# Moving table angles to GpSimd, a weight cast into its transfer and five relus to VectorE, with edge columns padded to 65, in a fused Fourier transform and feed-forward kernel

## The chip, the cores and the metric

The kernel runs on one core of one Trainium2 chip. The metric is the time of one execution on the device, in microseconds (us). The profile shows five engines of the core, each with its own instructions: PE (TensorE, matrix products; PEld is its weight load), DVE (VectorE), ACT (ScalarE), POOL (GpSimd), and SP, which here issues transfers (157 of 128 KB each to the output, among others). They run side by side: in the kernel before, the busy times of PE, DVE, ACT and POOL add up to 1691 us in a span of 628.5 us. All runs named below are on one core.

## The reference

```python
def reference(x, w_in, w_out):          # condensed; x (8, 3008, 256), w_in (256, 2048), w_out (2048, 256)
    X = np.fft.fft(np.fft.fft(x, axis=1), axis=2).real.astype(np.float32)
    h = np.maximum(X.reshape(-1, 256) @ w_in, 0.0)
    return (h * h @ w_out).astype(np.float32)
```

The real part of the transform is C x c - S x s, with cosine and sine matrices C and S over the 3008 positions and c and s over the 256 features. The kernel multiplies c and s into w_in once (G1, G2, G3), so only the transform over the positions is left to do for each of the eight batches, followed by two matrix products, the relu and the square.

## The kernel before

After some 50 us the kernel is a steady stream on PE (busy for 559.84 of the 560 us from 60 to 620 us, at a granted clock of 1.00): xb = G1 * pt + G2 * qt, a relu, a correction with G3, a second relu (both into h), a square, and po = h * wout. The change touches mainly the first 50 us, in which the tables are built and the first batch goes through. The tables are built in two blocks. Each block has two halves, and each half takes five operations on 128x564 elements, on VectorE:

```python
def nk():    vt(m, nval, krow, op=ALU.mult)                                   # L236
def near():  ts(out=t, in0=m, scalar1=1.0 / S, scalar2=R23, ...)              # L240
def turns(): ts(out=t, in0=t, scalar1=R23, scalar2=-float(S), ...)            # L244
def rest():  vt(m, m, t, op=ALU.add)                                          # L248
def size():  absval(t, m)                                                     # L183, on integers
# ... then sines on ScalarE give cosT and sinT, and mirrored columns follow (L279)
```

The second-layer weights arrive as float32 in a staging buffer, and VectorE casts them:

```python
for c in range(4):
    nc.gpsimd.dma_start(out=wot[c], in_=moe_w_out[...])
# ...
def wcast(c): nc.vector.tensor_copy(wout16[:, cs, :], wot[c])                 # L723
spread([(lambda c=c: wcast(c)) for c in range(4)], 3, 7)
spread(rd1[2:], 1, 8)          # the second block's angles
spread(fo, 7, 12)              # v, w: folding the first batch's odd features
# ... the second block's sines and cosines on ScalarE
spread(mi1, 9, 12)             # the second block's mirrored columns
spread(stage1_ops(0, 1, True), 11, 15)   # the second block's transform on PE
```

`spread(ops, lo, hi)` spreads operations over steps lo to hi of the main loop. Each step has one xb group. All relus into h are on ScalarE at this stage:

```python
def x_back(cur):
    # ... xb += G3 * qt
    relu_d(c, u, lambda o, i: act(o, xb[:, :, i], AF.Relu))
```

The edge column of batches 2 to 7 goes through the transform in matmuls with a stationary operand of three columns. There are eight groups of three of them:

```python
(nb, lambda q: eall[k, blk, q, bs[0] : bs[0] + nb], q, cosT)     # nb = 3
```

Of the kernel before, what the change touches and what calls it, by code (L numbers as in the profile page):

```python
# [10 lines left out]
F32 = mybir.dt.float32  # L11
F16 = mybir.dt.float16
I32 = mybir.dt.int32
AF = mybir.ActivationFunctionType
ALU = mybir.AluOpType
# [9 lines left out]
def kernel(  # L25
# [46 lines left out]
    def mm(o, l, r, start, stop):  # L72
        nc.tensor.matmul(o, l, r, start=start, stop=stop, skip_group_check=True)  # L73
# [59 lines left out]
    idx2 = iota("idx2", [P, 1], [[0, 1]], NQ // 2 * (NP - 1), -NQ // 2, I32)  # L133
    wout16 = const.tile([P, NFC, D], F16, name="wout16")
    wst = [h2p.tile([P, 2, F // 4], F32, name="wst", tag="h2") for _ in range(4)]
    wot = [h2p.tile([P, NFC // 4, D], F32, name="wot", tag="h2") for _ in range(4)]
    wS = 2.0 * math.pi / S
    wD = 2.0 * math.pi / D

# [50 lines left out]
    def dmats():  # L190
        pv = nc.gpsimd
        t = tgp.tile([P, P], F32, name="td", tag="td")
        m = tgp.tile([P, P], F32, name="md", tag="md")
        pv.tensor_scalar(out=m, in0=jrow, scalar1=pidx[:, 0:1], scalar2=None, op0=ALU.mult)
        pv.tensor_scalar(out=t, in0=m, scalar1=1.0 / D, scalar2=R23, op0=ALU.mult, op1=ALU.add)
        pv.tensor_scalar(out=t, in0=t, scalar1=R23, scalar2=-float(D),
                         op0=ALU.subtract, op1=ALU.mult)
        pv.tensor_tensor(m, m, t, op=ALU.add)
        pv.memset(csD[:, 0, 0, P - 1 : P], 1.0)

        def fin():
            absval(t, m)
            nc.vector.tensor_copy(csD[:, 0, 1, P - 1 : P], alt)
            act(csD[:, 0, 1, 0 : P - 1], m[:, 0 : P - 1], AF.Sin, bias=0.0, scale=wD)
            act(csD[:, 0, 0, 0 : P - 1], t[:, 0 : P - 1], AF.Sin, bias=hpi[:, 0:1], scale=-wD)

        def hi():
            ts(out=csD[:, 1, :, 0:P:2], in0=csD[:, 0, :, 0:P:2], scalar1=-1.0, scalar2=None,
               op0=ALU.mult)
            nc.vector.tensor_copy(csD[:, 1, :, 1:P:2], csD[:, 0, :, 1:P:2])  # L210
        return fin, hi

    cosT = const.tile([P, NQ, HE + HO], F16, name="cosT")
# [3 lines left out]
    def table_ops(blk):  # L217
        c0, n = BLK[blk]
        ng = (n + 1) // 2
        nm = n // 2  # L220
        cs = slice(c0, c0 + ng)
        tb = {}
        hq = NQ // 2
        kb = krow[:, blk : blk + 1, 0:ng].to_broadcast([P, hq, ng])

        def red(h):
            qs = slice(h * hq, (h + 1) * hq)

            def views():
                return tb["t"][:, qs, 0:ng], tb["m"][:, qs, 0:ng]  # L230

            def nk():
                if h == 0:
                    tb["t"] = tgp.tile([P, NQ, HG], F32, name="tt", tag="tt")
                    tb["m"] = tgp.tile([P, NQ, HG], F32, name="tm", tag="tm")
                vt(views()[1], nval[:, qs].unsqueeze(2).to_broadcast([P, hq, ng]), kb, op=ALU.mult)  # L236

            def near():
                t, m = views()
                ts(out=t, in0=m, scalar1=1.0 / S, scalar2=R23, op0=ALU.mult, op1=ALU.add)  # L240

            def turns():
                t, m = views()
                ts(out=t, in0=t, scalar1=R23, scalar2=-float(S), op0=ALU.subtract, op1=ALU.mult)  # L244

            def rest():
                t, m = views()
                vt(m, m, t, op=ALU.add)  # L248

            def size():  # L250
                t, m = views()
                absval(t, m)

            return [nk, near, turns, rest, size]

        def trig(h):
            qs = slice(h * hq, (h + 1) * hq)

            def cos(qs, bias):
                return lambda: act(cosT[:, qs, cs], tb["t"][:, qs, 0:ng], AF.Sin,  # L260
                                   bias=bias[:, 0:1], scale=-wS)

            def sin(qs, scale):
                return lambda: act(sinT[:, qs, cs], tb["m"][:, qs, 0:ng], AF.Sin, bias=0.0,
                                   scale=scale)

            if h == 0:
                return [sin(slice(0, hq, 2), wS), sin(slice(1, 2), wsh[:, 0:1]),
                        cos(slice(0, 1), hpe), cos(slice(1, 2), hph), cos(slice(2, 3), hpl)]
            return [sin(qs, wS), cos(qs, hpl)]  # L270

        src = slice(c0, c0 + nm)
        dst = slice(c0 + n - 1, c0 + n - 1 - nm, -1)

        def mir(d, a, qs, sv):
            o, i = d[:, qs, dst], (d if qs.start % 2 else a)[:, qs, src]
            if blk == 0:
                return lambda: act(o, i, AF.Copy, bias=0.0, scale=sv[:, 0:1])
            return lambda: ts(out=o, in0=i, scalar1=sv[:, 0:1], scalar2=None, op0=ALU.mult)  # L279

        qg = (slice(0, 5, 4), slice(2, 3), slice(1, 6, 4), slice(3, 4))
        return (red(0) + red(1), trig(0) + trig(1),
                [mir(cosT, sinT, qs, sv) for qs, sv in zip(qg, (nalt, alt, alt1, nalt))]
                + [mir(sinT, cosT, qs, sv) for qs, sv in zip(qg, (nalt, alt, nalt1, alt))])
# [27 lines left out]
        cs = slice(c * 512, (c + 1) * 512)  # L312
        ts(out=G3[:, cs], in0=G2[:, cs], scalar1=s3[:, 0:1], scalar2=None, op0=ALU.mult)

    eall = const.tile([P, 2, NQ, B], F16, name="eall")
    bf = {}
    INL = (0, 1)
    PQ = {}
# [86 lines left out]
    def stage1_ops(b, blk, inline_e=False, run=3):  # L405
# [30 lines left out]
                           (sgn[:, 0:1] if sn and inline_e else None, fin(sn)), run)  # L436
        return ops

    def e_ops(bs):
        nb = len(bs)  # L440

        def start():
            t = esp.tile([4, NK], F16, name="es", tag="es")
            for i, b in enumerate(bs):
                est[b] = (t, i)

        def fin(blk):
            def f(a, bp):
                lo_, hi_ = halves(blk, est[bs[0]][0][0:nb])
                vt(lo_, a, bp, op=ALU.add)  # L450
                vt(hi_, bp, a, op=ALU.subtract)
            return f

        ops = [start]
        for blk in range(2):
            ops += dft_ops(blk, lambda par, blk=blk: [
                (nb, lambda q: eall[k, blk, q, bs[0] : bs[0] + nb], q, cosT)
                for q in range(par, NQ, 2)], nb, (None, fin(blk)))
        return ops

# [24 lines left out]
    def plan(c, y, z):  # L485
        if chunks[c][1] != CH:
            return (), ()
        return ([u for u in range(NFC) if (u * y + 8) % NFC < y],
                [p for p in range(NFC // 2) if (p * z + 4) % (NFC // 2) < z])

    PLAN = [plan(c, *YZ[c]) for c in range(len(chunks))]

    gE = const.tile([P, NFC], F16, name="gE")
# [18 lines left out]
    def mm2_ops(c):  # L512
# [48 lines left out]
        def one(grp, j, fc):  # L561
            s, t0, m = grp[j]

            def f():
                if j == 0 and fc == 0:
                    st["o"] = pso.tile([P, 2, D], F32, name="po", tag="po")
                o = n + n % P + t0 if s == 1 else t0
                w = 2 * m if s == 2 else m
                mm(st["o"][0:w, j, :], h2v(c, fc // nf)[:, fc % (2 * nf), o : o + w], wout16[:, fc, :],
                   fc == 0 and j == 0, fc == NFC - 1)  # L570
                if fc == NFC - 1 and j == len(grp) - 1:
                    return lambda o=st["o"]: store(grp, o)
            return f
# [68 lines left out]
    def x_back(cur):  # L642
        c, u, xb = cur[:3]
        if xb is None:
            return
        g0, n, nf, segs = chunks[c]
        for j in range(nf):
            fs = slice((u * nf + j) * P, (u * nf + j + 1) * P)
            for (b, i, o, l) in segs:
                mm(xb[:, j, o : o + l], G3[:, fs], PQ[b][1][:, i : i + l], False, True)  # L650
        relu_d(c, u, lambda o, i: act(o, xb[:, :, i], AF.Relu))  # L651

    def x_square(cur):
# [19 lines left out]
                          in_=moe_w_in[:, cs].rearrange("(c p) f -> p c f", p=P))  # L673
    for c in range(4):
        nc.gpsimd.dma_start(
            out=wot[c], in_=moe_w_out[c * F // 4 : (c + 1) * F // 4, :].rearrange(
                "(c p) o -> p c o", p=P))
    for h in range(2):
        for f in rd0[5 * h : 5 * h + 5] + (tr0[5:] if h else tr0[:5]):
# [3 lines left out]
    dmats_fin()  # L683
    sgn_vecs()
    nc.vector.memset(ez, 0.0)
    for f in mi0 + fe[0:3] + rd1[0:2]:
        f()
    dmats_hi()
    warm = psx.tile([P, 512], F32, name="warm", tag="x")

    for _ in range(15):
        mm(warm, ez[:, 0, 0, :], ez[:, 0, 0:4, :], True, True)
    for f in fe[3:]:
        f()
    gcast(0, nc.scalar.copy)
    gmat(0)
    for _ in range(3):
        mm(warm, ez[:, 1, 0, :], ez[:, 1, 0:4, :], True, True)
    gcast(1, nc.scalar.copy)
    gcast(2, nc.vector.tensor_copy)  # L700
# [13 lines left out]
    def spread(ops, lo, hi):  # L714
        for i, f in enumerate(ops):
            side.setdefault(lo + int((hi - lo) * i / len(ops)), []).append(f)
# [1 line left out]
    for c in range(1, F // 512):  # L718
        side.setdefault(c * (c - 1) // 2, []).extend([lambda c=c: gmat(c), lambda c=c: gneg(c)])

    def wcast(c):
        cs = slice(c * NFC // 4, (c + 1) * NFC // 4)
        nc.vector.tensor_copy(wout16[:, cs, :], wot[c])  # L723

    spread([(lambda c=c: wcast(c)) for c in range(4)], 3, 7)
    spread(rd1[2:], 1, 8)
    spread(fo, 7, 12)
    spread(tr1[0:5], 5, 8)
    spread(tr1[5:], 8, 9)
# [111 lines left out]
```

## Time and profile before

| | before |
|---|---|
| median | 630.06 us (629.28 to 631.47, 4 runs) |
| span of the profiled run | 628.5 us |
| PE busy | 606.4 us, 96% |
| stretch in which PE is idle most, after the start | 30 to 42 us |

The busy time of the engines, from the first part of the page:

```profile
span 628.5 us, 11983 instructions
PE 606.4 (96%) x4682; PEld 446.9 (71%) x4682; DVE 536.8 (85%) x827; ACT 479.3 (76%) x872; POOL 68.8 (11%) x97
```

PE is the bottleneck, and outside the first 48 us it has no gap worth naming. So a gain must come from PE's own work, or from the gap early on. The windows view gives the gap. Its columns are the stretch in us, its length, the busy time of PE, PEld, DVE, ACT and POOL with the number of instructions, PE's granted clock, the busy share of the transfer engines and the GB/s:

```profile
36.00:38.00 2.00, 0.23 (x4) 0.10 (x2) 2.00 (x4) 2.00 (x4) 0.00 (x0) 1.00 0.74 191
38.00:40.00 2.00, 1.11 (x9) 0.60 (x8) 2.00 (x9) 2.00 (x5) 0.00 (x0) 1.00 0.30 37
40.00:42.00 2.00, 0.87 (x5) 0.43 (x4) 2.00 (x6) 0.76 (x2) 0.00 (x0) 0.56 0.02 0
42.00:44.00 2.00, 2.00 (x11) 1.32 (x9) 2.00 (x6) 0.60 (x1) 0.00 (x0) 0.50 0.10 0
44.00:46.00 2.00, 2.00 (x10) 1.18 (x9) 0.65 (x1) 0.60 (x1) 0.00 (x0) 0.50 0.03 0
46.00:48.00 2.00, 2.00 (x15) 1.53 (x14) 0.00 (x0) 0.74 (x2) 0.00 (x0) 0.73 0.00 0
```

VectorE is busy without a break until 44 us while PE waits. Some 2 us after the emptiest slice PE's clock falls to 0.5, so a PE that looks full from 42 us on does half the work: from the start of four po products to what follows them it takes 0.85 us there (43.00 to 43.85 us), and 0.44 us at the full clock (49.49 to 49.93 us). The busy times of the four are 1.06 and 0.60 us.

The timeline of PE shows the same stretch by instruction. Its columns are start, busy time, engine, line, operation, output and inputs, shapes and count; the brackets hold the idle time before and what ended it. `pf` is the transform of a block, and the one of 376 columns is the second block's:

```profile
22.18 0.27 PE L73 MATMUL xb<-qt,G 128*128 128x256 f16 x1 [0.68 <-DVE qt L423]
...
37.89 0.38 PE L73 MATMUL xb<-qt,G 128*128 128x256 f16 x2 [1.77 <-ACT h L605]
...
39.59 0.85 PE L73 MATMUL pf<-cosT,w 127*128 127x376 f16 x4 [0.89 <-DVE cosT L279]
41.57 0.78 PE L73 MATMUL pf<-cosT,w 127*128 127x376 f16 x2 [1.13 <-DVE cosT L279]
...
48.09 0.65 PE L73 MATMUL pf<-sinT,w 127*127 127x376 f16 x3
```

I call 22.18 us mark A (the first qt product), 39.59 us mark B (the second block's transform begins) and 48.09 us mark C (its first sine product). All kernels below have these three marks. The work of PE between them is the same, save where fillers are named, so the times between the marks can be compared from trace to trace.

PE waits for two engines here: from 28 to 46 us it waits 4.1 us for relus on ScalarE and 2.0 us for cosT from VectorE. The wait that ends last before mark B is the one for cosT. On VectorE, what stands before that cosT begins with the last absolute value of the angles, and VectorE does not pause from there to cosT (timeline of VectorE, same columns):

```profile
36.00 0.55 DVE L183 TENSOR_SCALAR tt<-tm 128x564 int32<-128x564 int32 x1
...
39.62 0.31 DVE L279 TENSOR_SCALAR cosT<-cosT,alt 128x376 f16<-128x376 f16 x1
```

Last, the edge groups, again on PE's timeline. The first row is a run of eight po products, the second an edge group with its three columns (127*3), and the third what follows:

```profile
369.12 1.03 PE L73 MATMUL po<-wout,h 128*128 128x256 f16 x8
370.08 0.64 PE L73 MATMUL pf<-cosT,eall 127*3 127x377 f16 x3
370.66 0.39 PE L73 MATMUL xb<-pt,G 128*128 128x512 f16 x1
```

The eight po products take 369.12 to 370.08, which is 0.96 us, and the edge group takes 0.58 us. No idle time is noted at either, and only a comparison with other groups shows that both are 0.1 us too long.

### The profile page before, as it was taken

Reading aid. Unit: us, or ns where it says so; the run is one execution under the profiler, and the core shown is the slowest. Engines: PE = TensorE matmul, PEld = TensorE weight load, DVE = VectorE, ACT = ScalarE, POOL = GpSimd, SP = SyncE. Lnnn points to the kernel's source line nnn. Section 1 sums busy time; section 2 is a strip of 40 time slices with the busy share of each in tenths; the row PEclk is TensorE's granted clock in tenths of the full one; section 3 lists DMA queues with packets and bytes.
Section 4 is the critical chain, followed back from the end, with each engine's and each line's share of the span. In section 5 each row is a group of like instructions: output and inputs, shape, how many; then the busy total and the mean of one; then the engine's idle time right before and its main releaser. Section 6 shows DMA issues by size and latency. Waiting matters only on the chain.

```text
span 628.5 us, 11983 instructions
## 1 busy us (share of the span) xinstructions
PE 606.4 (96%) x4682; PEld 446.9 (71%) x4682; DVE 536.8 (85%) x827; ACT 479.3 (76%) x872; POOL 68.8 (11%) x97
## 2 busy tenths in 40 slices
PE   3969999999999999999999999999999999999997
PEld 1547677776777777777777768777787778877786
DVE  8788799995988989889899879998999899999920
ACT  6768887777788788777887877877877778878871
POOL 8204043120120005000000000000000000000000
PEclk9979999999999999999999999999999999999999
DMA  8944477682591416714313314314233134131112
GB/s 282 300 83 138 120 181 205 156 225 57 91 208 36 59 44 170 138 34 59 43 51 44 57 34 63 43 47 48 54 56 43 51 43 59 52 46 48 52 52 68
DMA packets 37342, 57.21 MB, mean 91 GB/s; under 512 B 7262, under 2 KB 31490, under 8 KB 37286
## 3 DMA queue, kind: packets, MB, share of 16 engines
q0 software_dynamic: 7536, 30.21, 27.9%
q1 hardware_dynamic: 29702, 26.23, 13.4%
q8 instruction: 36, 0.59, 0.4%
q14 instruction: 20, 0.16, 0.1%
q10 hardware_dynamic: 48, 0.02, 0.0%
HBM read 29.02 MB, written 24.64 MB: 85 GB/s over the span
## 4 chain that ended last, share of the span: by engine, by line
PE 92%; DVE 6%; ACT 1%; issue 0%; DVEq 0%; POOL 0%; POOLq 0%; ACTq 0%
PE po L73 52%; PE xb L73 25%; PE pf L73 6%; PE xo L73 4%; PE xe L73 4%; DVE h L663 2%; PE warm L73 1%; DVE u L330 1%; DVE v L342 0%; DVE w L348 0%; DVE wout L723 0%; DVE tm L248 0%; ACT h L605 0%; DVE tm L236 0%; DVE tt L183 0%
## 5 line engine op out<-in xcount | busy, mean ns | idle before, releaser
L73 PE MATMUL po<-wout,h 128*128 128x256 f16 x3024 | 433.6, 273 | 0.0
L73 PEld LDWEIGHTS <-h 128*128 128x128 f16 x3024 | 287.2, 98 | 113.9 <-issue 0.4
L663 DVE TENSOR_TENSOR h<-h 128x2048 f16<-128x2048 f16 (+1 forms) x174 | 207.8, 1195 | 41.1 <-ACT h L651 36.5
L605 ACT ACTIVATE h<-xb 128x512 f16<-128x512 f32 (+1 forms) x270 | 159.2, 590 | 67.8 <-PE xb L73 67.1
L73 PE MATMUL xb<-qt,G 128*128 128x512 f16 (+11 forms) x720 | 203.6, 322 | 4.9 <-ACT h L605 4.1
L651 ACT ACTIVATE h<-xb 128x512 f16<-128x512 f32 (+2 forms) x286 | 160.4, 567 | 20.3 <-PE xb L73 13.9
L73 PEld LDWEIGHTS <-G 128*128 128x128 f16 x1384 | 130.3, 98 | 36.7 <-issue 9.6
L636 DVE CUSTOM_DVE_ANT_0 h<-xe,bs 128x512 f16<-128x512 f32 x228 | 145.9, 680 | 0.0
L73 PE MATMUL xb<-pt,G 128*128 128x512 f16 (+9 forms) x360 | 103.8, 324 | 0.3 <-DVE qt L424 0.2
L632 DVE SCALAR_TENSOR_TENSOR bs<-eb,gE,bs 128x512 f32<-128x512 f16 x114 | 85.0, 745 | 9.1 <-ACT bs L629 8.4
L629 ACT ACTIVATE bs<-xo 128x512 f32<-128x512 f32 x114 | 68.5, 601 | 21.0 <-PE xo L73 16.3
L557 ACT ACTIVATE os<-po 128x512 f32<-128x512 f32 x94 | 56.4, 600 | 19.1 <-PE po L73 16.7
L614 POOL DMA_DIRECT2D eb<-qt x28 | 15.4, 551 | 349.6 <-DVE bs L632 297.1
L73 PE MATMUL xo<-qt,G 128*128 128x512 f16 (+14 forms) x152 | 43.4, 327 | 0.0
L73 PE MATMUL xe<-pt,G 128*128 128x512 f16 (+14 forms) x152 | 43.4, 326 | 0.0
L330 DVE TENSOR_TENSOR u<-x 127x765 f16<-127x765 f32 x32 | 29.7, 945 | 0.0
L101 POOL DMA_INDIRECT x<-in_x_dram,idx x18 | 27.6, 1536 | 5.8 <-issue 4.5
L73 PEld LDWEIGHTS <-w 127*128 127x128 f16 (+1 forms) x192 | 21.6, 118 | 7.2 <-issue 1.4
L73 PE MATMUL pf<-cosT,w 127*128 127x377 f16 (+1 forms) x96 | 20.5, 327 | 2.0 <-DVE cosT L279 2.0
L124 POOL DMA_DIRECT2D x<-in_x_dram x14 | 7.9, 562 | 123.3 <-DVE u L334 122.7
L348 DVE TENSOR_TENSOR w<-v 127x381 f16<-127x381 f16 x64 | 20.7, 352 | 0.0
L73 PE MATMUL pf<-sinT,w 127*127 127x377 f16 (+1 forms) x96 | 20.7, 323 | 0.0
(103 smaller groups left out, 216.9 us busy)
## 6 DMA issues: line engine op xcount, KB each, us to landing
out_dram<-os SPq DMA_DIRECT2D x157, 128.0 KB
x<-in_x_dram POOLq DMA_DIRECT2D x14, 756.0 KB, 9.6
wst<-in_moe_w_in_dram POOLq DMA_DIRECT2D x4, 512.0 KB, 6.9
wot<-in_moe_w_out_dram POOLq DMA_DIRECT2D x4, 512.0 KB, 9.1
eb<-qt POOLq DMA_DIRECT2D x14, 128.0 KB, 6.7
x<-in_x_dram SPq DMA_DIRECT2D x2, 756.0 KB
x<-in_x_dram,idx POOLq DMA_INDIRECT x18, 10.7
gE<-G SPq DMA_DIRECT2D x16, 0.2 KB
```

The costliest lines, as they stand in the source:

```text
L73: nc.tensor.matmul(o, l, r, start=start, stop=stop, skip_group_check=True)
L101: nc.gpsimd.indirect_dma_start(out=x4[0:NP, 2 + s, q : q + rows, :].rearrange("p q d -> p (q d)"), out_offset=None, in_=bass.AP(tensor=x.t ...
L330: return lambda: vt(u[k, s, q0 : q0 + NQ // 2, 1:D], x4[k, s, q0 : q0 + NQ // 2, 1:D], x4[k, 3 - s, ::-1, :][:, q0 : q0 + NQ // 2, D - 1 : ...
L348: return lambda: vt(w[k, i, q : q + 3, 0 : P - 1], vs[s][k, q : q + 3, 1:P], vs[s][k, q : q + 3, D - 1 : P : -1], op=ALU.add if i < 2 else ...
L557: act(os_, po, AF.Copy, bias=0.0, scale=HS * HS)
L605: act(r_s(c, u), xb, AF.Relu)
L614: nc.gpsimd.dma_start(out=ebc[c][:, o : o + l], in_=PQ[b][1][P - 1 : P, i : i + l].unsqueeze(1).to_broadcast([1, P, l]))
L629: act(bs[0], xs[0], AF.Copy, bias=0.0, scale=1.0)
L632: stt(out=bs[1], in0=ebc[c][:, 0:n], scalar=gE2[:, u : u + 1], in1=bs[0], op0=ALU.mult, op1=ALU.subtract)
L636: nc.vector._custom_dve(TENSOR_ADD_SAT, out=o, in0=xs[1], in1=t, s0=BIG, s1=0.0)
L651: relu_d(c, u, lambda o, i: act(o, xb[:, :, i], AF.Relu))
L663: vt(h2, h2, h2, op=ALU.mult)
```

## The change

The intent is to relieve VectorE in the stretch 26 to 42 us, so that PE's gap closes, and to take away the short stops around the edge groups. The core of the diff, with the rest cut:

```diff
-    wot = [h2p.tile([P, NFC // 4, D], F32, name="wot", tag="h2") for _ in range(4)]
 ...  # csD's second half: two VectorE operations become two ScalarE operations
+        ve = nc.gpsimd if blk else nc.vector
 ...
-                vt(views()[1], nval[...], kb, op=ALU.mult)
+                ve.tensor_tensor(views()[1], nval[...], kb, op=ALU.mult)
 ...  # near, turns and rest likewise; size (the absolute value) stays on VectorE
-    eall = const.tile([P, 2, NQ, B], F16, name="eall")
+    MW = P // 2 + 1
+    eflat = const.tile([P, 2 * NQ * B + MW], F16, name="eall")
+    nc.gpsimd.memset(eflat, 0.0)
+    eall = eflat[:, 0 : 2 * NQ * B].rearrange("p (s q b) -> p s q b", s=2, q=NQ)
 ...
-                (nb, lambda q: eall[k, blk, q, bs[0] : bs[0] + nb], q, cosT)
+                (MW, lambda q: ewide((blk * NQ + q) * B + bs[0]), q, cosT)
 ...
-                w = 2 * m if s == 2 else m
+                w = MW if s == 2 else m
 ...
+    DRELU = ((1, 3, 5, 7), (1,))
+        if c < 2 and u in DRELU[c]:       # in x_back
+            relu_d(c, u, lambda o, i: ts(out=o, in0=xb[:, :, i], scalar1=0.0, ... op0=ALU.max))
+            return
 ...
-            out=wot[c], in_=moe_w_out[...]
+            out=wout16[:, c * NFC // 4 : (c + 1) * NFC // 4, :], in_=moe_w_out[...]
 ...
-    for f in mi0 + fe[0:3] + rd1[0:2]:
+    for f in mi0 + fe[0:3]:
-    for _ in range(15):                   # warm-up matmuls; further on, 3 become 2
+    for _ in range(13):
-    for f in fe[3:]:
+    for f in fe[3:] + rd1[0:4] + rd1[5:9]:
 ...
-    spread([(lambda c=c: wcast(c)) for c in range(4)], 3, 7)
-    spread(rd1[2:], 1, 8)
+    spread(rd1[4:5], 3, 4)
+    spread(rd1[9:], 6, 7)
```

Here rd1 holds the ten angle operations of the second block: 4 and 9 are the absolute values, which stay on VectorE, and the eight others go to GpSimd. fe folds the first batch's even features, and the loads of the second batch are issued in the middle of it.

More of the change, by code (lines that the diff above doesn't have):

```diff
@@ L207, in hi @@
         def hi():
-            ts(out=csD[:, 1, :, 0:P:2], in0=csD[:, 0, :, 0:P:2], scalar1=-1.0, scalar2=None,
-               op0=ALU.mult)
-            nc.vector.tensor_copy(csD[:, 1, :, 1:P:2], csD[:, 0, :, 1:P:2])
+            act(csD[:, 1, :, 0:P:2], csD[:, 0, :, 0:P:2], AF.Copy, bias=0.0, scale=-1.0)
+            nc.scalar.copy(csD[:, 1, :, 1:P:2], csD[:, 0, :, 1:P:2])
         return fin, hi
@@ L235, in nk @@
                     tb["m"] = tgp.tile([P, NQ, HG], F32, name="tm", tag="tm")
-                vt(views()[1], nval[:, qs].unsqueeze(2).to_broadcast([P, hq, ng]), kb, op=ALU.mult)
+                ve.tensor_tensor(views()[1], nval[:, qs].unsqueeze(2).to_broadcast([P, hq, ng]), kb,
+                                 op=ALU.mult)
             def near():
                 t, m = views()
-                ts(out=t, in0=m, scalar1=1.0 / S, scalar2=R23, op0=ALU.mult, op1=ALU.add)
+                ve.tensor_scalar(out=t, in0=m, scalar1=1.0 / S, scalar2=R23, op0=ALU.mult, op1=ALU.add)
             def turns():
                 t, m = views()
-                ts(out=t, in0=t, scalar1=R23, scalar2=-float(S), op0=ALU.subtract, op1=ALU.mult)
+                ve.tensor_scalar(out=t, in0=t, scalar1=R23, scalar2=-float(S), op0=ALU.subtract,
+                                 op1=ALU.mult)
             def rest():
                 t, m = views()
-                vt(m, m, t, op=ALU.add)
+                ve.tensor_tensor(m, m, t, op=ALU.add)
             def size():
@@ L437, in stage1_ops, with ewide @@
         return ops
+    def ewide(o):
+        return eflat[k, o : o + MW]
     def e_ops(bs):
@@ L650, in x_back @@
                 mm(xb[:, j, o : o + l], G3[:, fs], PQ[b][1][:, i : i + l], False, True)
+        if c < 2 and u in DRELU[c]:
+            relu_d(c, u, lambda o, i: ts(out=o, in0=xb[:, :, i], scalar1=0.0, scalar2=None,
+                                         op0=ALU.max))
+            return
         relu_d(c, u, lambda o, i: act(o, xb[:, :, i], AF.Relu))
@@ L675 @@
         nc.gpsimd.dma_start(
-            out=wot[c], in_=moe_w_out[c * F // 4 : (c + 1) * F // 4, :].rearrange(
+            out=wout16[:, c * NFC // 4 : (c + 1) * NFC // 4, :], in_=moe_w_out[c * F // 4 : (c + 1) * F // 4, :].rearrange(
                 "(c p) o -> p c o", p=P))
@@ L696 @@
     gmat(0)
-    for _ in range(3):
+    for _ in range(2):
         mm(warm, ez[:, 1, 0, :], ez[:, 1, 0:4, :], True, True)
@@ L719 @@
         side.setdefault(c * (c - 1) // 2, []).extend([lambda c=c: gmat(c), lambda c=c: gneg(c)])
-    def wcast(c):
-        cs = slice(c * NFC // 4, (c + 1) * NFC // 4)
-        nc.vector.tensor_copy(wout16[:, cs, :], wot[c])
-    spread([(lambda c=c: wcast(c)) for c in range(4)], 3, 7)
-    spread(rd1[2:], 1, 8)
+    spread(rd1[4:5], 3, 4)
+    spread(rd1[9:], 6, 7)
     spread(fo, 7, 12)
```

## The prediction

> **What bounds it now.** The page gives PE 606.4 us busy of a 628.5 us span. From 48 us on PE is continuously busy at the full granted clock (busy time by stretches), so what leaves VectorE or ScalarE there is worth nothing. What can be won:
> - PE starts at 10.92 us, after the memset of ez, with 15 + 3 warm-ups, about 0.43 us apart[...].
> - Between 30 and 42 us PE is busy for only 5.8 of 12 us; VectorE is busy throughout, ScalarE from 23 to 41 (timeline). The chain there runs wout cast, tm, tt, square, ..., v, square, cosT, then the second block's DFT on PE at 39.6. The waits give PE 6.8 us (4.1 for relus, 2.0 for cosT, 0.7 for qt).
> - After that gap the granted clock is 0.5 from about 40.4 to 47, costing some 3 us.
> - Each of the eight groups of three edge matmuls (3 columns wide) has 0.09 us of extra start-to-start time before it and 0.10 us behind it; 127-column groups have none. The 16-column group at 615.5 us too, 0.2 us.[...]
>
> **What the change does.**
> - 65 columns: removes those gaps, 8 x 0.19 + 0.2..0.4 = about 1.8 us, all on PE's path. The larger weight load hides behind a 158 ns matmul.
> - Start: 0.78 us of csD work goes to ScalarE, 1.3 us of angles leave VectorE's front; but w_in's arrival (14.7 us) and the ScalarE casts hold the first stage. Fewer warm-ups: about 0.5 us.
> - VectorE, 26 to 42 us: loses four casts (2.7) and angle steps (about 3.9), gains five relus at an estimated 0.6 (3.0): net -3.6. ScalarE loses five relus, about -2.5.
> - GpSimd gains eight operations of 564 elements a partition. Its 128-element ones took 0.62 to 0.88 us.[...] They stand behind the loads of x(1), the last of which ended at 22.6 us after waiting for a w_out transfer[...]. Before, the second was ready at 36.0. So GpSimd probably becomes the wait that ends last, and part of VectorE's relief is lost: relus follow in order behind it.
>
> **Sum.** Edges -1.8, start -0.5, gap 30 to 42 us -2.5, low clock -1.5 (an even chance of -3). About -6 us: **624.0 us**, 8 in 10 within 618.5 to 630. Faster by over 2%: 0.07; within 2%: 0.90; slower by over 2%: 0.03.
>
> **To check.** [...]the second DFT block starts near 37 to 38; relus on VectorE cost 0.6 us; no gap at edge groups; the clock has a shorter 0.5 stretch or none; after 60 us the traces run parallel.
>
> **What would make it wrong.** GpSimd at 3 us or more an operation: VectorE waits in order, PE starves until 45 to 50 us, several us slower. A casting transfer that lands late delays GpSimd's start and the first second-layer matmuls (35.5 us). Better: the gap closes and the clock never drops, 618.

Passages are cut from it where marked. -1.8 - 0.5 - 2.5 - 1.5 comes to -6.3, put as about -6, and 630.06 less 6 is the 624.0. But the -2.5 allows for a wait for GpSimd, and the prediction does not say how much. The 0.6 us of a relu on VectorE is an estimate, with no source named; in the kernel before, VectorE's operations from 128x512 in PSUM took 0.68 us (L636) and ScalarE's relus 0.59 us (L605).

## The result, and the profile after

The kernel after takes 627.13 us (median of 4 runs, 626.72 to 627.61). The ratio to before is 0.9946, with a 95% interval of 0.993 to 0.9962. A ratio is the mean time of one kernel's runs over that of the other's of the same rounds, so it is not quite the ratio of the medians. The gain is 2.9 us where about 6 were predicted. The time lies within the predicted range, but half of the expected gain is missing.

The profiled run has a span of 625.3 us, 3.2 us less. PE's timeline at the marks:

```profile
21.46 0.27 PE L73 MATMUL xb<-qt,G 128*128 128x256 f16 x1 [0.68 <-DVE qt L427]
...
36.70 0.38 PE L73 MATMUL xb<-qt,G 128*128 128x256 f16 x2 [2.49 <-ACT h L613]
...
39.59 1.41 PE L73 MATMUL pf<-cosT,w 127*128 127x376 f16 x4 [2.08 <-DVE cosT L280]
41.57 0.78 PE L73 MATMUL pf<-cosT,w 127*128 127x376 f16 x2 [0.57 <-DVE cosT L280]
...
46.84 0.65 PE L73 MATMUL pf<-sinT,w 127*127 127x376 f16 x3
```

Mark A comes 0.72 us earlier, but mark B comes at 39.59 us in both kernels. Relative to the start, the way to mark B has become 0.72 us longer. From B to C it takes 7.25 us instead of 8.50, and from C to the end 578.5 instead of 580.4. So the 3.2 us come from the start (-0.7), from B to C (-1.25) and from the rest (-1.95), with +0.7 in between.

Why mark B stands still can be read from VectorE's timeline:

```profile
34.81 0.55 DVE L182 TENSOR_SCALAR tt<-tm 128x564 int32<-128x564 int32 x1 [1.52 <-POOL tm L249]
35.27 0.68 DVE L660 TENSOR_SCALAR h<-xb 128x512 f16<-128x512 f32 x1
...
38.09 0.68 DVE L660 TENSOR_SCALAR h<-xb 128x512 f16<-128x512 f32 x1
...
39.62 0.31 DVE L280 TENSOR_SCALAR cosT<-cosT,alt 128x376 f16<-128x376 f16 x1
```

VectorE stands idle for 1.52 us until GpSimd has its last angles ready, and starts the last absolute value at 34.81 us, 1.19 us earlier than before. From there to the third mirrored cosT it then takes 39.62 - 34.81 = 4.81 us instead of 39.62 - 36.00 = 3.62 us, again 1.19 us. Two of the relus that moved to VectorE stand in between, each holding the next operation back by 0.6 us. The relu at 35.27 us also started only behind the absolute value, although PE had started no product for any xb since 33.50 us and VectorE stood idle in the meantime. What the relief brought, the relus took back to the hundredth.

The windows view of the same stretch:

```profile
34.00:36.00 2.00, 0.21 (x2) 0.04 (x1) 1.19 (x3) 1.19 (x2) 0.78 (x1) 1.00 0.90 165
36.00:38.00 2.00, 0.81 (x6) 0.48 (x5) 2.00 (x4) 2.00 (x5) 0.00 (x0) 0.92 0.71 171
38.00:40.00 2.00, 0.41 (x2) 0.35 (x3) 2.00 (x10) 0.11 (x1) 0.00 (x0) 0.50 0.18 17
40.00:42.00 2.00, 1.43 (x6) 0.56 (x5) 2.00 (x6) 0.48 (x1) 0.00 (x0) 0.50 0.03 0
42.00:44.00 2.00, 2.00 (x11) 1.32 (x9) 2.00 (x6) 0.60 (x1) 0.00 (x0) 0.50 0.03 0
44.00:46.00 2.00, 2.00 (x17) 1.50 (x16) 1.24 (x2) 0.65 (x2) 0.00 (x0) 0.88 0.00 0
```

The stretch at half the clock is no shorter than before. What is missing to a clock of 1.00 adds up to 2 us x (0.44 + 0.50 + 0.50 + 0.27) = 3.42 us before and 2 us x (0.08 + 3 x 0.50 + 0.12) = 3.40 us after. At half the clock that is 6.8 us in both. It only lies earlier, so more of it falls into time in which PE waits anyway, and that is the gain between B and C. How much of this the change brought about is not shown: the kernel edge_only, below, has a B to C shorter by 0.69 us than before, although nothing that runs up to mark C was changed in it but a memset at the start.

GpSimd's share, on its timeline, from the second operation of the second half on:

```profile
29.62 0.67 POOL L240 TENSOR_SCALAR tt<-tm 128x564 f32<-128x564 f32 x1
30.37 2.94 POOL L244 TENSOR_SCALAR tt<-tt 128x564 f32<-128x564 f32 x1
33.40 1.38 POOL L249 TENSOR_TENSOR tm<-tm,tt 128x564 f32<-128x564 f32 x1
```

GpSimd is done at 34.8 us, and of its operations the one at L244 is by far the longest.

The edge groups have lost their stops (the same three rows of PE's timeline as shown of before): the po run before one takes 0.87 us now (367.77 - 366.90) and the group 0.49 us (368.26 - 367.77).

```profile
366.90 1.04 PE L73 MATMUL po<-wout,h 128*128 128x256 f16 x8
367.77 0.65 PE L73 MATMUL pf<-cosT,eall 127*65 127x377 f16 x3
368.26 0.38 PE L73 MATMUL xb<-pt,G 128*128 128x512 f16 x1
```

### The profile page after: what moved, and what is told of

Its sections match the earlier page's. It is cut to its first block, busy times and chain, and to the rows that moved or that the text cites. A ratio compares the mean times of both kernels' runs of the same rounds, so it can differ in the third digit from the quotient of the medians.

```text
span 625.3 us, 11976 instructions
## 1 busy us (share of the span) xinstructions
PE 602.1 (96%) x4679; PEld 448.3 (72%) x4679; DVE 536.1 (86%) x818; ACT 477.0 (76%) x869; POOL 79.6 (13%) x106
## 3 DMA queue, kind: packets, MB, share of 16 engines
q0 software_dynamic: 9072, 29.16, 28.0%
## 4 chain that ended last, share of the span: by engine, by line
PE 90%; POOL 4%; DVE 3%; DMA 1%; issue 1%; ACT 0%; DVEq 0%; POOLq 0%; ACTq 0%
PE po L73 52%; PE xb L73 25%; PE pf L73 5%; PE xe L73 4%; PE xo L73 4%; DMA wout<-in_moe_w_out_dram 1%; DVE h L675 1%; POOL tt L244 1%; DVE u L334 1%; POOL x L101 0%; POOL wst L684 0%; POOL tm L249 0%; DVE w L352 0%; DVE v L346 0%; POOL tm L235 0%
## 5 line engine op out<-in xcount | busy, mean ns | idle before, releaser
L663 ACT ACTIVATE h<-xb 128x512 f16<-128x512 f32 (+2 forms) x281 | 156.8, 565 | 20.0 <-PE xb L73 13.5
L398 ACT ACTIVATE as<-pf 128x377 f32<-128x377 f32 (+5 forms) x32 | 15.5, 484 | 8.8 <-PE pf L73 8.6
```

What stands on the lines that cost most here:

```text
L398: act(st["a"][0:m, :], st[0][0:m, :], AF.Copy, bias=0.0, scale=1.0 if fin[0] is None else fin[0])
```

## The experiments

Twelve kernels ran, each timed in five rounds (six runs) beside the kernel before, whose median was 629.7 to 630.3 us in all of these jobs. The jobs ran on three chips, so between jobs the ratio is the safer comparison. The table has all of them. A, B, C and the end are read from each profiled run; "half clock" is the time that PE's granted clock was 0.5 after 30 us, worked out from the windows view in steps of 0.2 us.

| kernel | median us | ratio (95%) | A | A to B | B to C | C to end | half clock |
|---|---|---|---|---|---|---|---|
| before | 630.06 | 1 | 22.18 | 17.41 | 8.50 | 580.4 | 6.83 |
| after | 627.13 | 0.9946 (0.993 to 0.9962) | 21.46 | 18.13 | 7.25 | 578.5 | 6.83 |
| edge_only | 628.63 | 0.998 (0.9964 to 0.9996) | 21.78 | 17.41 | 7.81 | 578.6 | 6.83 |
| free_angles | 623.6 | 0.9901 (0.988 to 0.9921) | 21.96 | 14.61 | 7.37 | 578.5 | 3.41 |
| early_angles | 626.91 | 0.9955 (0.9933 to 0.9977) | 24.63 | 14.62 | 7.24 | 578.4 | 3.42 |
| fill_gap | 626.57 | 0.995 (0.9935 to 0.9964) | 21.93 | 18.96 | 4.95 | 578.5 | 0 |
| no_relu | 627.9 | 0.9972 (0.9951 to 0.9993) | 22.11 | 17.03 | 8.02 | 578.4 | 6.82 |
| wcast_v | 630.09 | 1.0006 (0.9987 to 1.0025) | 21.62 | 20.25 | 6.52 | 578.4 | 10.24 |
| angles_vector | 628.23 | 0.9974 (0.9956 to 0.9993) | 22.22 | 16.41 | 8.54 | 578.4 | 6.83 |
| three_step | 627.3 | 0.9961 (0.9942 to 0.9979) | 23.96 | 15.00 | 7.51 | 578.4 | 3.42 |
| three_b1 | 627.24 | 0.9956 (0.9934 to 0.9978) | 21.43 | 16.81 | 8.52 | 578.4 | 6.83 |
| late_wout | 626.49 | 0.9943 (0.9918 to 0.9968) | 22.32 | 16.14 | 7.50 | 578.4 | 3.42 |
| cast_edge | 624.24 | 0.9907 (0.9889 to 0.9926) | 22.31 | 15.52 | 5.45 | 578.4 | 0 |
| no_gp_no_relu | 624.0 | 0.9901 (0.9882 to 0.992) | 22.63 | 15.53 | 5.45 | 578.4 | 0 |

The theories: (1) GpSimd's angles come late, VectorE waits for them in order, and this eats the relief. (2) The relus that moved to VectorE eat it. (3) The low clock is what the time hangs on, and a gap that closes a little does not help. (4) The gain is the edges' alone and the rest is worth nothing.

### edge_only: the padding alone, on the kernel before

```diff
-    eall = const.tile([P, 2, NQ, B], F16, name="eall")
+    eflat = const.tile([P, 2 * NQ * B + MW], F16, name="eall")      # and so on, as in the change
-                w = 2 * m if s == 2 else m
+                w = MW if s == 2 else m
```

> The kernel before with the 65-column padding alone. Theory: the two traces differ by 1.25 us up to the same matmul group near 48 us and by 3.2 us at the end, and only the edge groups differ behind it, so the padding alone should give about -1.9 us (ratio 0.997). Rival: the padding is worth nothing and the later 1.9 us came from something else; then 1.000.

Measured: 628.63 us, ratio 0.998, so some 1.3 us by the ratio and 1.6 by the medians. In the trace, the time from mark C to the end, where all edge groups lie, goes from 580.4 to 578.6 us. All other kernels with the padding have 578.4 or 578.5 there. So the padding is worth 1.8 to 2.0 us in the trace, as predicted, and theory 4 accounts for no more than about two thirds of the 2.9 us.

This run shows one thing more. Up to mark C it does the same work as the kernel before, and A to B takes the same 17.41 us. But here the clock falls 0.8 us before mark B, and in the kernel before it falls 0.65 us after that mark, so more of the low stretch lies in PE's waits, and B to C takes 7.81 us instead of 8.50:

```profile
39.19 1.44 PE L73 MATMUL pf<-cosT,w 127*128 127x376 f16 x4 [0.89 <-DVE cosT L279]
...
47.00 0.65 PE L73 MATMUL pf<-sinT,w 127*127 127x376 f16 x3
```

So 0.7 us between B and C can come and go with the place of the low stretch alone.

### free_angles: the second block's angles left out

```diff
+                if blk:
+                    tb.update(TB0)        # take the first block's angles
+                    return
```

> The changed kernel with the eight GpSimd operations of the second block left out (the second block takes the first block's angles, so the result is wrong on purpose; everything else stays, the absolute values on VectorE too). Theory A (GpSimd is the wait that ends last, and while it runs VectorE's operations are stretched): the 1.5 us wait of VectorE near 33 us goes, and the multiply to G3, the w_in cast and the absolute value return to about 0.35, 0.7 and 0.55 us; 3 to 4 us less idle time on PE before 42 us, so 2.5 to 5 us faster than the changed kernel, near 623. Rival B (the five relus that VectorE took on are what eats the gain, GpSimd is harmless): less than 1 us.

This kernel's result is wrong (relative error 0.639), and it shows what the angles cost wherever they are done. Measured: 623.6 us. The way from A to B falls by 3.5 us against after. Its trace also shows something that the prediction had left out. Several of VectorE's operations, the same in both kernels, are shorter here, where GpSimd does no angles. Two of them in the kernel after:

```profile
22.23 1.98 DVE L299 CAST win<-wst 128x1024 f16<-128x1024 f32 x1
...
28.46 1.48 DVE L182 TENSOR_SCALAR tt<-tm 128x564 int32<-128x564 int32 x1
```

The same two in free_angles:

```profile
22.73 0.69 DVE L310 CAST win<-wst 128x1024 f16<-128x1024 f32 x1
...
28.28 0.54 DVE L182 TENSOR_SCALAR tt<-tm 128x564 int32<-128x564 int32 x1
```

With three multiplications to G3 (0.74, 0.55 and 1.02 us against 0.35 each) and one square (1.49 against 1.21), VectorE loses 3.8 us between 22 and 32 us while GpSimd works. The relus that read PSUM are not stretched (0.68 us in both; the ones at 25.54 and 31.28 us in the kernel after ran while GpSimd worked), and neither was a second square, at 32.06 us (1.23 us in both). Why some operations grow and others do not is not shown.

### early_angles: GpSimd does the angles before it issues the loads of the second batch

```diff
-    for f in fe[3:] + rd1[0:4] + rd1[5:9]:
+    for f in rd1[0:4] + rd1[5:9] + fe[3:]:
```

> The changed kernel with the GpSimd angle operations ahead of the loads of x(1) instead of behind them, so that they start near 15 us. Theory A: the wait near 33 us goes, but the contention moves onto the folding of x(0) on VectorE and delays the first DFT stage by 1 to 2 us; net between -2 and +1 us against the changed kernel. If contention is no cost at all: -2 to -3 us. If the waits are harmless (B): no gain, only the delay.

Measured: 626.91 us (624.7 to 629.1), not told apart from after. GpSimd ended at 28.4 us instead of 34.8, and VectorE waited for it no more: A to B fell to 14.62 us, as in free_angles. But VectorE's operations were now stretched at the start: two folding operations that take 1.82 us in the kernel after took 2.99, and mark A came at 24.63 us, 3.2 us late, of which 0.8 us is a later arrival of the second part of the first batch. So the wait can be taken away, but GpSimd's work cost VectorE time in both places tried.

### fill_gap: matmuls of no use in the gap, to hold the clock

```diff
+        if si == FILL[0]:
+            filler(FILL[1])               # 12 matmuls of 376 columns
 ...                                       # the step's G3 correction and square
+        if si == FILL[0]:
+            filler(FILL[2])               # 12 more, before the step's side work
```

> The changed kernel with 12 + 12 filler matmuls of 376 columns (about 0.16 us each) in the two places where PE idles 2.1 to 2.5 us before the second DFT block; their output is overwritten. Theory: the low clock from 38 to 44 us follows from this idleness; with PE kept busy the granted clock stays 1.0 and the kernel gains 2 to 3 us (near 624.5). Rival: the clock is lowered for another reason or the fillers cost more than they save: 0 or slower.

Measured: 626.57 us, ratio 0.995, not told apart from after. The clock stayed at 1.0 in the profiled run and at 0.997 to 1.0 in all six, and B to C fell from 7.25 to 4.95 us. Of these 2.3 us a shorter wait for cosT is 0.28 (0.29 instead of 0.57), so the low clock cost about 2.0 us there. But the fillers themselves had to wait, 1.75 us, until a relu on VectorE was done, and mark B came later (18.96 us after A). Theory 3 is right here: the low clock has a price of this size, and it did not come when PE was kept busier (1.58 and 2.00 us of the two slices from 36 to 40 us, where it was 0.81 and 0.41 in after). But useless work in the gap did not get it back.

### no_relu: the change without relus on VectorE

```diff
-    DRELU = ((1, 3, 5, 7), (1,))
+    DRELU = ((), ())
```

> The changed kernel with all relus back on ScalarE. If VectorE ends the chain (relus stand behind its wait for GpSimd), taking 5 x 0.6 us off it gains 1 to 2 us, near 625.5; if ScalarE is the tighter of the two before 36 us, it loses 1 to 2 us, near 628.5.

Measured: 627.9 us, ratio 0.9972; the difference from after lies within the intervals. A to B falls by 1.1 us and B to C rises by 0.8 us. VectorE now stands idle for 1.9 us before the last absolute value, until GpSimd is done. Taking the relus away alone is no gain: in this kernel theory 1 holds.

### wcast_v: the change with the cast of w_out on VectorE as before

```diff
-            out=wout16[:, c * NFC // 4 : (c + 1) * NFC // 4, :], in_=moe_w_out[...]
+            out=wot[c], in_=moe_w_out[...]
+    spread([(lambda c=c: wcast(c)) for c in range(4)], 3, 7)
```

> The changed kernel with w_out loaded as it is and cast by VectorE as before. The four casts (0.6 us each) return to VectorE between 28 and 36 us, where it waits 1.5 us for GpSimd: 0.5 to 2 us slower than the changed kernel. Side question, from the trace: x(0) and w_in landed about 0.5 us later in the changed kernel; if the casting transfer delays them, they land earlier here and part of the loss is won back.

Measured: 630.09 us, ratio 1.0006. The whole gain is gone, the edges' included. VectorE is busy for 19.5 of the 20 us from 28 to 48 us, mark B comes 20.25 us after A, and the clock is low for 10.24 us. The four casts take 1.62, 0.99, 1.26 and 0.68 us, where they took 0.68 each before: the first three start while GpSimd works, which is until 34.9 us.

### angles_vector: the change with all angles on VectorE

```diff
-        ve = nc.gpsimd if blk else nc.vector
+        ve = nc.vector
 ...                                       # and the places in the program as before
```

> The changed kernel with the second block's angles back on VectorE at the places of the kernel before. Removes VectorE's 1.5 us wait and some 3.8 us of stretching by GpSimd, and adds 8 operations, 5.2 us, to VectorE, of which about 1.3 us stand where VectorE waits for x(0) anyway. If the GpSimd move was about a wash, within 1 us of the changed kernel; if it was worth what VectorE was relieved of, 3 to 5 us slower.

Measured: 628.23 us, ratio 0.9974. It has the relus on VectorE and no angles on GpSimd. Mark B comes 16.41 us after A, 1.7 us better than after, but B to C takes 8.54 us with the clock low for 6.83. So GpSimd is not the only thing that takes the relief back: theory 1 alone does not explain the missing gain.

### three_step, three_b1 and late_wout: less work for GpSimd, later transfers

three_step counts the angles in turns, so that three operations do for four, in both blocks. three_b1 does so in the second block only. late_wout is three_b1 with the casting transfers held back until a later transfer of w_in has landed.

```diff
-            def turns():
-                ...                       # dropped; near subtracts R23 again in the same operation
+                ve.tensor_scalar(out=t, in0=m, scalar1=R23, scalar2=R23, op0=ALU.add, op1=ALU.subtract)
```

> The changed kernel with the angles counted in turns, so that each half block needs three operations instead of four (the one that took 2.1 and 2.9 us on GpSimd goes, in block one also on VectorE). Theory A (wait for GpSimd and stretching of VectorE): GpSimd ends near 30 instead of 34.8 us, VectorE's wait at 33 us goes and its stretch is about half, so 2 to 3 us faster than the changed kernel, near 624.5. If GpSimd is not what bounds: no change.

> The changed kernel with the three-operation angles in block one alone, so that the start stays as it was (in the run three_step the start had changed too: PE stood idle 2.0 us before w_in came and ran its first DFT stage at the low clock, which hid what the shorter GpSimd work gave). Theory A: start as in the changed kernel, GpSimd done near 31 to 32 us, no wait of VectorE at 33 us; 1.5 to 2.5 us faster than the changed kernel, near 625. If the GpSimd wait is not what bounds: no change.

> three_b1 with w_out's casting transfers held on GpSimd until the second quarter of w_in has landed, the angles behind them, and the loads of x(1) last. Theory: x(0) and w_in no longer share the transfers with w_out, land 0.5 to 1.5 us earlier, and VectorE's early relief becomes usable; GpSimd ends near 28 us: 1 to 2 us faster than three_b1. Rival: the folding of x(0) meets GpSimd at work and is stretched, as in early_angles: slower than three_b1.

Measured: 627.3, 627.24 and 626.49 us; none is told apart from after. three_step upset the start (PE idle for 2.02 us before w_in, mark A at 23.96 us), so it says little of the gap. three_b1 is the clean one. GpSimd ended at 32.5 us, VectorE did not wait for it, and A to B fell by 1.32 us against after. B to C rose by 1.27 us, and the total stayed. The clock was low for 6.83 us as before, but now more of it fell on PE's work. So a gain in the gap can be paid back behind it while the clock drops for the same time. How much is paid back hangs on where the low stretch falls too: it began 0.7 us after mark B here and 1.9 us before it in after.

late_wout shows what the clock is worth, since its six runs differ in it: 624.7 and 625.2 us at a mean clock of 1.0, 626.2 and 626.8 at 0.997, 628.3 and 628.4 at 0.996 and 0.995. The mean clock is no measure by itself: in wcast_v the two fastest runs, 628.6 and 629.4 us, have the two lowest clocks, 0.991 and 0.989, and the slowest, 630.95 us, has 0.995.

### cast_edge: the padding and the casting transfer alone, on the kernel before

```diff
 # the kernel before, and of the change only:
+    eflat, MW and ewide                   # the padding
+            out=wout16[:, c * NFC // 4 : (c + 1) * NFC // 4, :], in_=moe_w_out[...]
-    spread([(lambda c=c: wcast(c)) for c in range(4)], 3, 7)
```

> The kernel before with the 65-column padding and the casting transfer alone: VectorE loses the four casts (2.7 us) in the stretch where it is busy without a pause, nothing else moves. If those casts lie on the chain, 1.5 to 2.7 us less than edge_only, near 626.5, which would make this as fast as the whole change; if ScalarE binds there, less than 1 us.

Measured: 624.24 us (623.87 to 625.33), ratio 0.9907. Half of the change gives twice the gain. The clock was 0.999 or 1.0 in all six runs. Against edge_only this is the transfer's part alone: 4.4 us by the medians, for four casts of 0.68 us that leave VectorE. Mark B no longer waits for cosT: the last wait of PE before it is 0.94 us for a relu on ScalarE, here and in no_gp_no_relu, so ScalarE is next in line.

### no_gp_no_relu: the change without angles on GpSimd and without relus on VectorE

```diff
 # angles_vector, and:
-    DRELU = ((1, 3, 5, 7), (1,))
+    DRELU = ((), ())
```

> The change with the second block's angles on VectorE and with no first relus on VectorE; it differs from the kernel with all angles on VectorE (628.2 us) only in the five relus, which go back to ScalarE, and from the kernel with padding and casting transfer alone (624.2 us) only in the csD copies on ScalarE and in three warm-ups fewer. Theory A, the relus take the place on VectorE that the casting transfer had freed, and the clock drops again for that: 624.2 give or take 0.8, the second DFT block at about 37.8 us instead of 39 to 40, and no stretch at half the clock in most runs. Rival B, the warm-ups and csD copies at the start cost it (a late first stage[...]): 627.5 to 628.5, a stretch at half the clock after 38 us, and the second block's DFT not before 38.5.

Measured: 624.0 us (623.37 to 624.99), ratio 0.9901, and a clock of 0.999 or 1.0 in all six runs. It beats both kernels, and it is not told apart from cast_edge. The fewer warm-ups and the csD copies on ScalarE, which it has and cast_edge has not, are thus worth nothing that these runs show (mark A is even 0.3 us later). PE's timeline:

```profile
22.63 0.27 PE L73 MATMUL xb<-qt,G 128*128 128x256 f16 x1 [0.68 <-DVE qt L427]
...
38.16 0.81 PE L73 MATMUL pf<-cosT,w 127*128 127x376 f16 x4
39.75 0.48 PE L73 MATMUL pf<-cosT,w 127*128 127x376 f16 x2 [0.79 <-DVE cosT L280]
...
43.61 0.65 PE L73 MATMUL pf<-sinT,w 127*127 127x376 f16 x3
```

VectorE's timeline, with the same two operations as above, 3.62 us apart as in the kernel before:

```profile
34.19 0.55 DVE L182 TENSOR_SCALAR tt<-tm 128x564 int32<-128x564 int32 x1
...
37.81 0.31 DVE L280 TENSOR_SCALAR cosT<-cosT,alt 128x376 f16<-128x376 f16 x1
```

And the windows view:

```profile
36.00:38.00 2.00, 1.06 (x11) 0.80 (x9) 2.00 (x8) 2.00 (x5) 0.00 (x0) 1.00 0.70 157
38.00:40.00 2.00, 1.21 (x9) 0.71 (x8) 2.00 (x6) 2.00 (x5) 0.00 (x0) 1.00 0.27 40
40.00:42.00 2.00, 2.00 (x19) 1.64 (x18) 2.00 (x7) 1.46 (x3) 0.00 (x0) 1.00 0.09 0
```

The last absolute value starts earlier than in the kernel after, although VectorE does all the angles itself. PE is busy for over 1 us in every slice of 2 us from 34 us on, and the clock does not drop.

Together with three kernels above, this makes a square of the two disputed moves. All four have the casting transfer, the padding and the change's start:

| | relus on ScalarE | five relus on VectorE |
|---|---|---|
| angles on VectorE | 624.0 (no_gp_no_relu) | 628.2 (angles_vector) |
| angles on GpSimd | 627.9 (no_relu) | 627.1 (after) |

Either move costs about 4 us on its own (4.6 and 4.5 by the ratios), and the two together about 3. Why they do not add up can be read from the profiled runs, but was not tested further. With neither move there is no stretch at half the clock; with one or both there are the same 6.83 us of it. That is one loss, and it is paid once: B to C is 3.1 us longer in angles_vector, 2.6 in no_relu and 1.8 in after, where 2.6 more are lost from A to B and 1.2 won before A.

## Why the prediction was right or wrong

**The bound.** Right. VectorE and ScalarE hold the gap, with VectorE's cosT as the wait that ends last before mark B, and PE's gap with the low clock behind it is what can be won early on. The marks show it: everything after mark C differs by the edges alone.

**Edges, -1.8 us.** Right in the trace: C to the end falls by 1.95 us in the kernel after. In time, edge_only gave 1.3 to 1.6. With 65 columns in place of three, the eight po products before a group take 0.09 us less (0.87 for 0.96) and the group 0.09 us less (0.49 for 0.58). The wider weight load costs nothing that shows: the three loads of a group are busy for 0.38 us (0.25 with three columns), within the group's 0.49, at 0.16 us a matmul. Why the narrow operand costs this time was not shown.

**Start, -0.5 us.** Measured -0.72 at mark A, right in size. The warm-ups are not its cause, since no_gp_no_relu and angles_vector have the fewer warm-ups too, and have mark A at 22.2 to 22.6. Kernels without the second block's angles at VectorE's front (no_relu, free_angles, fill_gap, wcast_v) have it at 21.6 to 22.1, so it may come from there, but edge_only has 21.8 with those angles in place. So small a part was not settled.

**Gap of 30 to 42 us, -2.5 us.** This is the step that failed. Mark B stayed at 39.59 us, where 37 to 38 was predicted, and came 0.72 us later relative to A. Of the sum "loses four casts (2.7) and angle steps (about 3.9), gains five relus at an estimated 0.6 (3.0): net -3.6" the single numbers were good: a relu took 0.68 us and held back the next operation by 0.6. The fault was to set off busy times against each other. What counts is the chain to the second block's cosT. On it, the last absolute value came only 1.19 us earlier (0.47 relative to A), since it waited for GpSimd, and two relus put 1.19 us back. The casts were the piece of relief that worked: alone with the padding, they bring mark B to 15.52 us after A (17.41 before), which is -1.9 of the predicted -2.5. The rest of the change undid this.

**GpSimd as the wait that ends last.** Right: its operations ended at 28.4 and 34.8 us, and VectorE waited 1.52 us for the second half. Measured, the two-input ones took 1.14 to 1.38 us, and the one at L244, with one input, 2.10 and 2.94 us, even though the one-input operation at L240 took 0.67 to 0.98. What the prediction missed altogether is that VectorE's operations on SBUF took longer while GpSimd worked, by 3.8 us in sum against free_angles. Some of it fell into VectorE's idle time, so it is not 3.8 us of the total.

**Low clock, -1.5 us.** B to C gave -1.25 us, but that the number fits is luck: the stretch, predicted as shorter or gone, is as long as before (6.83 us in both) and only lies more in idle time, and edge_only had -0.69 there without any change of the gap. The part that was left open, "an even chance of -3", is what separates this kernel from 624 us. In cast_edge and no_gp_no_relu the stretch is gone, and B to C falls from 8.50 to 5.45 us, of which 0.34 are a shorter wait and 2.7 the clock.

**The sum.** The predicted 624.0 is what the relief gives when it reaches the chain: cast_edge has 624.24 and no_gp_no_relu 624.0. Their traces give -1.9 for A to B, -3.05 for B to C and -2.0 for the edges, and +0.1 and +0.45 at the start. That 624.0 comes out so exactly is luck in part: these kernels make neither the move of the angles (-3.9 on VectorE by the sum) nor that of the relus (+3.0), and they gain 3.05 us from B to C where -1.5 was predicted for the clock.

**What stays open.** Which pattern of idle time makes the clock drop was not tested, and the traces do not settle it. The low stretches after 30 us lasted 3.41 to 3.42, 6.82 to 6.83 or 10.24 us, so I take PE's busy time in stretches of 3.41 us, a length chosen for that reason alone, counted back from where the clock fell (windows view). In the eleven profiled runs with a low stretch, PE was busy for 0.81 to 1.63 us of the last 3.41 us before the fall (1.47 before, 0.81 after, 1.63 in free_angles), and for 1.67 us or more in each of the two stretches ahead of it, after which the clock stayed up. In the three runs that kept the clock, the emptiest 3.41 us after 24 us had 1.63 us of busy time (cast_edge and no_gp_no_relu) and 1.54 (fill_gap). These ranges overlap, so the busy time of such a stretch alone does not tell the runs apart, and the kernels that kept the clock lie among values at which it fell elsewhere. One kernel can do either: of free_angles' six runs four were at 0.999 or 1.0 and two at 0.997. early_angles has one run at a clock of 1.0 that took 628.4 us, which nothing here explains. Whether the moves of angles and relus can be placed so that they help was not tried; only that they do not help as they stand.

## What to carry to other kernels

When work is moved off a busy engine, follow the chain to the operation that the bottleneck waits for, and count what stands on it afterwards, rather than adding busy times over a stretch; here, two operations of 0.6 us put into the freed place took back all of the relief at mark B. Move one thing at a time, and try the change's parts alone: here half of the change gave 6 us and the whole 2.9. Where a gap is followed by a low clock, watch the clock of each run, because here a shorter gap without the clock saved (three_b1) gave nothing that the runs show, and two kernels that saved it (cast_edge and no_gp_no_relu) gained twice as much as the whole change.

## What the traces show of the hardware

- VectorE beside GpSimd: VectorE's operations on SBUF grew from 0.69 to 1.98 us (float32 to float16 cast), from 0.54 to 1.48 (integer absolute value) and from 0.35 to 1.02 (multiplication by a column) while GpSimd worked (free_angles and after); in wcast_v a cast of w_out grew from 0.68 to 1.62. The relus from PSUM did not grow (0.68 in both), nor did one square (1.23 in both).
- GpSimd's operations on 128x564 float32, in the kernel after: 1.38 us for the addition of two tensors and 1.14 to 1.19 for the multiplication. Those with scalars, of the same shape, differ threefold: 0.67 to 0.98 us (multiply, add) and 2.10 to 2.94 us (subtract, multiply); in three_b1 one that adds and subtracts took 2.10 and 2.64 us. Why is open.
- PE's clock: the stretches at 0.5 after 30 us lasted 0, 3.41 to 3.42, 6.82 to 6.83 or 10.24 us in the fourteen profiled runs, and nothing in between. It fell after 0.81 to 1.63 us of busy time in 3.41 us (see what stays open). The granted clock differs between runs of one kernel too: late_wout had mean clocks from 0.995 to 1.0, and its time went from about 625.0 to 626.5 and 628.4 us with them.
- Edge groups: a group of three matmuls with a stationary operand of three columns cost 0.18 us more than one with 65 columns, 0.09 before it and 0.09 within it up to the next matmul.
- Casting transfers: they landed a piece after 9.3 us, where without a cast a piece had 9.1 us (both medians of four, and both read 512 KB; the cast writes 256), and the queue that carried them had 9072 packets instead of 7536. So the cast saved VectorE's time, and nothing here shows that it saved time of the transfer.
